# Another hand-written order for the first 18 head pairs of a fused attention and feed-forward kernel

## The chip, the core and the metric

The kernel runs on one core of a Trainium2 chip. A core has five engines that run their own instruction queues in order: TensorE (PE; its weight loads are shown as PEld), VectorE (DVE), ScalarE (ACT), GpSimd (POOL) and SyncE (SP, which here only issues DMAs). Matrix products are written to PSUM, a memory of eight banks; everything else lies in SBUF, 128 partitions wide. The metric is the time of one execution in microseconds (us).

## The reference

Cosine attention over 8 batches of 12 heads (448 tokens, 64 features a head), then a feed-forward layer on its result.

```python
q_n = q / (norm(q, axis=-1) + 1e-06)
k_n = k / (norm(k, axis=-1) + 1e-06)
attn = softmax((q_n @ k_n^T) / tau)          # tau = 0.1
x = (attn @ v), heads side by side           # 3584 x 768
h = x @ w_in                                 # 768 x 2048
out = (h * clip(h + 3, 0, 6) / 6) @ w_out    # 2048 x 768
```

## The kernel before

Two heads of one batch make a *pair* i (0 to 47), two pairs a *twin* d. What is loaded at a time is an *item* j: all q or all k of a twin, 128 partitions x 896 numbers (item 2d and 2d+1). Up to pair 17 everything that the program does stands in `PLAN` (L21 to L58), a list of lines of short codes; `run` (L959) takes them one by one and each code appends its instructions to the queue of its engine. So the list fixes the order within each engine's queue and nothing between engines, which wait for each other by semaphores alone. From pair 18 on a loop (L998 and following) writes the order; it is the same before and after.

The codes, with their lines:

- `LQ.j` loads an item, `LV.d` the values of a twin in four DMAs (both on SP). `W` (L909) issues one of eight loads of feed-forward weights, 768 KB each, from POOL's queue: four of w_in, then four of w_out.
- `SQ.j.e.c.n` squares n of an item's 7 columns (14 for items 0 and 1) on engine e: a is ACT (L222), v VectorE, p POOL (L224). `RE.j` adds the squares up (VectorE, L236). `NO.d` (L252 to L255) makes 1/(norm + 1e-6) of a twin in four small ACT operations: ln, exp(0.5 x), ln(x + 1e-6), exp(-x). `NM.j.e` multiplies the item by it and writes bf16 (L267). Squares lie in two buffers: items j and j+2 share one.
- `TR.j` turns an item in seven TensorE transposes into a bank (L312); from item 14 on `XD.j` does it by DMA (L323). `CQ.i`, `CK.i`, `CS.i` copy a pair's q, its k and the k of the last 64 tokens to where the score product reads them (L334 on VectorE, L332 on ACT, L362 on VectorE and L372 on POOL for DMA-turned items).
- `SC.i.g` is a group of score products (L412, L415), four groups a pair: three of 2 x 448 columns and a smaller one. `EX.i.g` is exp of it on ACT (L433). `VC.i` casts the values (L286, or L284 on VectorE as a reduction over one element), `VA.i.g` multiplies them with the exponentials into the bank pair PV (L455), and `FI.i` divides by the sums (VectorE, L475 and L476). `BK.i` and `CX.i` turn the result and copy it to the feed-forward input xT; `XB` and `XP` do it by DMA.
- `U` (L932) issues TensorE's next feed-forward unit from a list of 36: thirty of six products with w_in (L566, `mm1_unit`) and six output units of sixteen products with w_out (L613, `mm2_unit`). `UA` and `UV` issue the ACT and the VectorE part that follow a unit (L575, L581, L624, L626); the last of them gives the unit's bank back.
- `WS.x` adds or subtracts blocks of w_out (VectorE, L688). The sums 1, 6 and 7 have tiles of their own; y3 and y4 overwrite w_out in place, so they come after the sums that read it and after the output units. The products of the loop need them.
- `D.n` and `DP.n` issue n products with zeros, of 512 columns into bank Y (L916) and of 248 columns into an unused part of PV (L921). Nothing reads them.
- `OPEN` changes the PSUM layout: up to there scores alternate between two two-bank tiles; behind it scores, units, transposes and `BK` take banks in turn from a ring of six. An operation that takes a bank waits until whoever read it last is done.

Of the kernel before, what the change touches and what calls it, by code (L numbers as in the profile page):

```python
# [10 lines left out]
AF = mybir.ActivationFunctionType  # L11
# [3 lines left out]
EPS = 1e-6  # L15
# [3 lines left out]
ORDER = "111111111111111111111111111111222222"  # L19

PLAN = [  # L21
# [36 lines left out]
]  # L58


# [1 line left out]
def kernel(  # L62
# [10 lines left out]
    nc = tc.nc  # L73
    B, H, S, D = q.shape
# [29 lines left out]
    KC = FCN // 2  # L104
# [34 lines left out]
    def raw_buffer(j):  # L139
# [4 lines left out]
    n2s = [const.tile([128, 2, 14], FP32, name=f"n2{i}", tag=f"n2{i}") for i in range(2)]  # L144
    rs = [
        [const.tile([128, 2, 14], FP32, name=f"{x}{i}", tag=f"{x}{i}") for x in ("ln", "nr", "le", "r")]
        for i in range(2)
    ]
# [13 lines left out]
    engines = {"v": nc.vector, "p": nc.gpsimd, "a": nc.scalar, "s": nc.sync}  # L162
    issued = set()

    def needs(*what):
        for w in what:
            assert w in issued or any(x < 0 for x in w[1:] if isinstance(x, int)), w
# [76 lines left out]
    def norms(d, *items):  # L244

        needs(("NM", 2 * d - 4), ("NM", 2 * d - 3))
        items = items or (0, 1)
        for x in items:
            needs(("RE", 2 * d + x))
        it = slice(items[0], items[-1] + 1)  # L250
        ln, nr, le, r = (t[:, it, :] for t in rs[d % 2])
        nc.scalar.activation(out=ln, in_=n2s[d % 2][:, it, :], func=AF.Ln)  # L252
        nc.scalar.activation(out=nr, in_=ln, func=AF.Exp, scale=0.5)
        nc.scalar.activation(out=le, in_=nr, func=AF.Ln, bias=EPS)
        nc.scalar.activation(out=r, in_=le, func=AF.Exp, scale=-1.0)  # L255
        for x in items:
            issued.add(("NO", d, x))

# [411 lines left out]
            return wide[n % 2], wide[2]  # L670
        return wide_late[2 * (n - LOOP) : 2 * (n - LOOP) + 2]

    def weight_sums(what, c0, n):

        w = w_out_sb[:, :, :].rearrange("p (c k) m -> p c k m", k=2)[:, c0 : c0 + n]
        b11, b12, b21, b22 = (w[:, :, k, m] for k in range(2) for m in (LEFT, RIGHT))
        for x in {"y3": "16", "y4": "17"}.get(what, ""):
            assert all((x, c) in summed for c in range(c0, c0 + n))
        o, x, y, op = {
            "1": (b11, b11, b22, ALU.add),  # L680
            "6": (b11, b11, b12, ALU.add),
            "7": (b21, b21, b22, ALU.add),
            "y3": (b12, b12, b22, ALU.subtract),
            "y4": (b21, b21, b11, ALU.subtract),
        }[what]
        if what in w_sum:
            o = w_sum[what][:, c0 : c0 + n, :]
        nc.vector.tensor_tensor(out=o, in0=x, in1=y, op=op)  # L688
        summed.update((what, c) for c in range(c0, c0 + n))

    def half(b, t, k):
# [247 lines left out]
    def whole_units(n, engines="av"):  # L939
# [4 lines left out]
                    finish_units(e)  # L944

    OPS = {
        "LQ": load_qk, "LV": load_v, "W": next_weights, "SQ": square, "RE": reduce, "NO": norms,
        "NM": normalise, "VC": vcast, "TR": transposes, "XD": crossbar, "XB": back_crossbar, "XP": back_two, "CQ": copy_q, "CK": copy_k, "CS": copy_k3, "SC": scores,
        "EX": exps, "VA": values, "FI": finish_values, "BK": back, "CX": copy_x, "U": unit, "UA": lambda: finish_units("a"), "UV": lambda: finish_units("v"),
        "GL": g_left, "WS": lambda x, *h: weight_sums(str(x), *((h[0] * KC // 2, KC // 2) if h else (0, KC))), "UU": whole_units, "D": busy, "DP": busy_pv, "OPEN": open_ring,  # L950
    }

    def do(op, *args):
        OPS[op](*args)
        key = (op,) + tuple(a for a in args if isinstance(a, int))
        if op not in ("RE", "NM", "LQ"):
            issued.add(key[:3] if op == "SC" else key)

    def run(text):  # L959
# [36 lines left out]
    for i in range(FIRST, NP):  # L996
# [36 lines left out]
        n = 2  # L1033
# [59 lines left out]
```

## Time and profile before

| what | us |
|---|---|
| median of 3 runs (405.66 to 406.52) | 406.1 |
| the profiled execution | 405.02 |
| its span, first to last instruction | 403.2 |
| PE busy | 394.5 |
| VectorE / ACT / POOL busy | 286.4 / 266.2 / 233.2 |
| 86 zero products `DP`, between 2.5 and 41.6 | 13.3 by their durations, which overlap |
| 10 zero products `D`, from 5.71 | 2.3 |
| first exponential / first feed-forward unit start | 12.11 / 42.1 |
| last output unit of the planned part ends | 114.3 |

The granted TensorE clock was 1.00 in every stretch. Durations of PE overlap, since products are pipelined: the distance between two starts is the price of one. On the other engines the distance between two starts is a little below a duration as well. A line of the timeline gives start, length, engine, line, operation, output and input tiles, count, and in brackets the idle time before it with what ended it. A line of the waits gives who waited for whom, the total, the number of times and the longest.

### The profile page before, as it was taken

Reading aid. Unit: us, or ns where it says so; the run is one execution under the profiler, and the core shown is the slowest. Engines: PE = TensorE matmul, PEld = TensorE weight load, DVE = VectorE, ACT = ScalarE, POOL = GpSimd, SP = SyncE. Lnnn points to the kernel's source line nnn. Section 1 sums busy time; section 2 is a strip of 40 time slices with the busy share of each in tenths; the row PEclk is TensorE's granted clock in tenths of the full one; section 3 lists DMA queues with packets and bytes.
Section 4 is the critical chain, followed back from the end, with each engine's and each line's share of the span. In section 5 each row is a group of like instructions: output and inputs, shape, how many; then the busy total and the mean of one; then the engine's idle time right before and its main releaser. Section 6 shows DMA issues by size and latency. Waiting matters only on the chain.

```text
span 403.2 us, 9617 instructions
## 1 busy us (share of the span) xinstructions
PE 394.5 (98%) x3696; PEld 233.7 (58%) x3696; DVE 286.4 (71%) x501; ACT 266.2 (66%) x609; POOL 233.2 (58%) x228
## 2 busy tenths in 40 slices
PE   7999999999989999999999999999999999999996
PEld 5666556555655556555555556555565556555564
DVE  6898768766998676776857878687656666644663
ACT  6899998787557686776758768668648755224230
POOL 7899664562294996489386875776665500510070
PEclk9999999999999999999999999999999999999999
DMA  8999989989989559885989659986864523130133
GB/s 290 308 241 276 200 249 239 144 126 221 193 204 231 120 119 228 176 224 130 181 214 210 134 143 171 183 193 145 191 150 82 112 46 67 40 79 20 27 73 99
DMA packets 91566, 65.32 MB, mean 162 GB/s; under 512 B 56064, under 2 KB 89984, under 8 KB 91520
## 3 DMA queue, kind: packets, MB, share of 16 engines
q1 hardware_dynamic: 87408, 58.02, 62.8%
q0 software_dynamic: 3712, 6.29, 9.1%
q8 instruction: 29, 0.48, 0.5%
q10 hardware_dynamic: 400, 0.39, 0.3%
q14 instruction: 17, 0.14, 0.1%
HBM read 47.19 MB, written 11.01 MB: 144 GB/s over the span
## 4 chain that ended last, share of the span: by engine, by line
PE 94%; DVE 3%; DMA 1%; POOL 1%; ACT 0%; issue 0%; SPq 0%; DVEq 0%
PE M L566 24%; PE M L739 17%; PE PV L455 13%; PE Y L566 6%; PE M L415 6%; PE Z L566 5%; PE Y L739 4%; PE Z L739 4%; PE M L613 3%; PE M L819 2%; PE Z L415 2%; PE PV L921 2%; PE Z L819 1%; PE Y L415 1%; PE SC L415 1%; DMA big<-in_q_dram 1%
## 5 line engine op out<-in xcount | busy, mean ns | idle before, releaser
L433 ACT ACTIVATE at<-M 128x448 bf16<-128x448 f32 x200 | 99.6, 565 | 17.7 <-PE M L415 15.5
L566 PE MATMUL M<-xT,w_in_sb 128*128 128x448 bf16 x522 | 110.7, 353 | 0.0
L566 PEld LDWEIGHTS <-w_in_sb 128*128 128x128 bf16 x768 | 71.9, 98 | 62.5 <-issue 2.6
L267 POOL TENSOR_TENSOR nrm<-big,r 128x896 bf16<-128x896 f32 (+1 forms) x48 | 79.4, 1658 | 26.7 <-ACT r L255 18.5
L581 DVE SCALAR_TENSOR_TENSOR gT<-u,M 128x448 bf16<-128x448 bf16 x76 | 46.8, 618 | 35.6 <-ACT u L575 35.3
L455 PEld LDWEIGHTS <-at 128*128 128x128 bf16 (+1 forms) x1536 | 54.8, 97 | 24.1 <-issue 14.8
L224 POOL TENSOR_TENSOR big<-big 128x896 f32<-128x896 f32 (+3 forms) x39 | 63.8, 1639 | 8.0 <-DMA big<-in_k_dram 4.1
L575 ACT ACTIVATE u<-M 128x448 bf16<-128x448 f32 x87 | 48.8, 561 | 29.5 <-PE M L566 29.1
L455 PE MATMUL PV<-vx,at 128*128 128x65 bf16 (+1 forms) x1536 | 64.3, 194 | 0.2 <-DVE on L476 0.2
L236 DVE TENSOR_REDUCE n<-big 128x14 f32<-128x896 f32 (+1 forms) x50 | 51.8, 1040 | 3.9 <-ACT big L222 3.4
L372 POOL COPY km<-tT 64x128 bf16<-64x128 bf16 x34 | 12.4, 364 | 59.3 <-DMA tT<-nrm 43.4
L768 POOL TENSOR_TENSOR big<-big 128x384 f32<-128x384 f32 x11 | 12.0, 1088 | 55.1 <-ACT big L787 55.0
L739 PEld LDWEIGHTS <-gT 128*128 128x128 bf16 x288 | 27.8, 98 | 20.2 <-DVE gT L717 0.6
L739 PE MATMUL M<-w_out_sb,gT 128*128 128x384 bf16 x208 | 37.9, 326 | 0.1
L433 ACT ACTIVATE at<-Z 128x448 bf16<-128x448 f32 x49 | 27.6, 564 | 10.4 <-PE M L415 8.8
L286 POOL CAST vx<-big 128x512 bf16<-128x512 f32 x44 | 33.0, 754 | 2.4 <-DMA big<-in_v_dram 2.4
L476 DVE TENSOR_TENSOR on<-PV,rc 128x512 bf16<-128x512 f32 x48 | 33.2, 691 | 1.7
L415 PE MATMUL M<-tT,kz 64*128 64x448 bf16 (+1 forms) x175 | 31.9, 351 | 1.0 <-DVE o L626 1.0
L739 PEld LDWEIGHTS <-gs 128*128 128x128 bf16 x224 | 21.6, 98 | 14.5
L566 PE MATMUL Y<-xT,w_in_sb 128*128 128x448 bf16 x132 | 28.6, 353 | 0.0
L433 ACT ACTIVATE at<-Y 128x448 bf16<-128x448 f32 x45 | 25.6, 568 | 3.3 <-PE Z L415 3.1
L739 PE MATMUL M<-w_sum,gs 128*128 128x384 bf16 x144 | 26.3, 326 | 0.0
(131 smaller groups left out, 553.9 us busy)
## 6 DMA issues: line engine op xcount, KB each, us to landing
big<-in_v_dram SPq DMA_DIRECT2D x96, 128.0 KB, 4.7
big<-in_k_dram SPq DMA_DIRECT2D x24, 448.0 KB, 4.9
big<-in_q_dram SPq DMA_DIRECT2D x24, 448.0 KB, 4.3
out_dram<-o SPq DMA_DIRECT2D x107, 96.0 KB, 2.2
w_in_sb<-in_moe_w_in_dram POOLq DMA_DIRECT2D x4, 768.0 KB, 9.1
w_out_sb<-in_moe_w_out_dram POOLq DMA_DIRECT2D x4, 768.0 KB, 9.7
tT<-nrm SPq DMA_TRANSPOSE x34, 3.4
xT<-on SPq DMA_TRANSPOSE x25, 3.8
```

Of the source, the lines that this page charges most:

```text
L224: engines[e].tensor_tensor(out=o, in0=i, in1=i, op=ALU.mult)
L236: nc.vector.tensor_reduce(out=n2s[d % 2][:, j % 2, c], in_=sq[:, :, :, :].rearrange("p g c d -> p (g c) d")[:, c, :], axis=AX.X, op=ALU.add,)
L267: engines[e].tensor_tensor(out=nrm[:, :, g, :].rearrange("p c g d -> p g c d"), in0=raw_of[j][:, g, :, :], in1=rs[d % 2][3][:, j % 2, :] . ...
L286: (engines[e].copy if e == "a" else engines[e].tensor_copy)(out=o, in_=f)
L415: nc.tensor.matmul(o, ks, qt[rows], start=True, stop=True)
L433: nc.scalar.activation(out=o, in_=x, func=AF.Exp, scale=inv_tau)
L455: nc.tensor.matmul(pv_out(j, h), at[rows, n, q_cols(i // HP, j)], vt[rows, 3 + h if name == "M" else 5 * h + int(name[1]), :], start=(name ...
L476: nc.vector.tensor_tensor(out=on[:, :, :, :].rearrange("p j h d -> p h j d"), in0=pv4[:, :, :, 0:D], in1=rc[:, :, :].to_broadcast([128, 2, ...
L566: nc.tensor.matmul(ps[:, 0:S], w_in_sb[:, cc, fc * 128 : (fc + 1) * 128], x[:, cc, 0:S], start=(cc == 0), stop=(cc == CC - 1),)
L575: nc.scalar.activation(out=u[:, :], in_=ps[:, 0:S], func=AF.Relu, bias=0.5, scale=1.0 / 6.0)
L581: nc.vector.scalar_tensor_tensor(out=g[:, fc, c0 : c0 + S], in0=u[:, :], scalar=1.0, in1=ps[:, 0:S], op0=ALU.min, op1=ALU.mult,)
L739: nc.tensor.matmul(m, lhs[:, c, :], rhs[:, c, c0 : c0 + width], start=(base is None and c == 0), stop=(c == KC - 1), skip_group_check=True,)
```

## The change

`PLAN` is written anew, 37 lines for 36: the same steps for pairs 0 to 17 in another order, and in part on other engines or in other pieces.

- Zero products `DP`: 64 for 86, all of them ahead of `SC.2.0`; the group `D.10` opens the list.
- Squares: 30 pieces for 29 (11, 15 and 4 on ACT, POOL and VectorE for 12, 14 and 3). Item 1 is squared whole on ACT, item 0 by ACT (9 columns) and POOL (5); items 4, 7 and 10 go to VectorE; item 14 is squared in seven pieces of one column on three engines.
- Twins 2 to 6 get `NA.d` (the first two ACT operations of `NO`: ln, exp) and `ND.d` (an addition of 1e-6 and a reciprocal, on VectorE). They are new functions.
- Three of the four half normalisations of items 0 and 1 go to VectorE, and item 13's; items 2 and 18 return to POOL.
- On ACT instead of VectorE or POOL: four `CK`, five `CQ`, one `CS`, three `CX` (one, one, none and one before), and three casts `VC`; ten casts on POOL for sixteen.
- Of the weight sums, `WS.1` and `WS.7` and `WS.6` are made in halves, one half of each on POOL; y3 in two halves on VectorE.
- `TR.10` stands before the first `U`; `SC.17.3` behind the last.

The functions and the plan, the old one cut to its first lines and to those of its end:

```diff
 PLAN = [
-    "LQ.1 DP.5 SQ.1.a.11.3 SQ.1.p.4.3 DP.1 SQ.1.a.0.4 LQ.0 SQ.0.p.8.6 DP.2 DP.4 LQ.3 LQ.2 SQ.1.v.7.4 RE.1.1",
-    "SQ.0.a.0.6 RE.1.0 NO.0.1 LQ.5 LQ.4 SQ.0.v.6.2 DP.6 SQ.3.a.0.7 NM.1.p.0 D.10 RE.0.1 DP.3 NM.1.p.1 RE.0.0 DP.8",
-    "NO.0.0 LV.0 DP.2 SQ.2.a.0.7 NM.0.p.0 RE.3 RE.2 NM.0.p.1 TR.1.Y DP.2 TR.0.Z CK.0.v DP.4 SQ.4.p.0.7 CQ.0.v",
...
-    "CK.17.v XD.18 U EX.16.1 SQ.20.a.0.7 NM.19.p FI.15 WS.6 U UV XD.19 SC.16.3 RE.20 GL.0 WS.1 WS.7.0 EX.16.2 U VA.16.0 UA VA.16.1 LV.11",
-    "EX.16.3 SC.17.0 UV VC.19.p SC.17.1 SC.17.2 SQ.22.v.0.7 VA.16.2 LQ.23 EX.17.0 VA.16.3 EX.17.1 LV.10 U SC.17.3",
-    "XP.14 NO.10 FI.16 NM.20.p CK.18.v U CK.19.v WS.7.1 WS.y3 WS.y4.0 XB.16 EX.17.2 UV UA VA.17.0 VC.18.p EX.17.3 RE.22 CS.18.v",
+    "D.10 DP.9 LQ.1 SQ.1.a.0.14 DP.10 LQ.0 LQ.3 LQ.2 SQ.0.p.9.5 RE.1.1 SQ.0.a.0.9 RE.1.0 RE.0.1 RE.0.0 NO.0.1",
+    "DP.10 NM.1.v.0 NM.1.v.1 NO.0.0 NM.0.p.0 NM.0.v.1 TR.1.Y LQ.5 TR.0.Z DP.7 SQ.3.a.0.7 SQ.2.a.0.7 RE.3 DP.5",
+    "SQ.5.p.0.7 CK.1.a CK.0.a RE.2 CQ.0.a CQ.1.a NO.1 SC.0.0.0 SC.0.1.1 EX.0.0 NM.2.p NM.3.p DP.8 EX.0.1 SC.0.2.0",
+    "LQ.4 DP.6 LV.0 SC.0.3.1 DP.1 EX.0.2 SQ.4.v.0.7 RE.5 SC.1.0.0 TR.2.Z EX.0.3 RE.4 LQ.7 NA.2 VC.1.v EX.1.0",
+    "SC.1.1.1 VC.0.v VA.0.0 EX.1.1 LQ.6 TR.3.Y SQ.6.a.0.7 ND.2 SQ.7.v.0.7 SC.1.2.0 VA.0.1 VA.0.2 EX.1.2 NM.4.p",
+    "CQ.2.v LV.1 CK.2.v SC.1.3.1 NM.5.p CK.3.a VA.0.3 CQ.3.v DP.8 RE.6 LQ.8 EX.1.3 SC.2.0.0 FI.0 SC.2.1.1 LQ.9",
+    "EX.2.0 TR.4.Y VA.1.0 SC.2.2.0 VA.1.1 VC.2.v VA.1.2 EX.2.1 EX.2.2 SQ.8.p.0.7 LQ.10 RE.7 VA.1.3 VC.3.p",
+    "SQ.9.p.0.7 SC.2.3.1 SC.3.0.0 FI.1 NA.3 CQ.4.a TR.5.Z EX.2.3 ND.3 SC.3.1.1 VA.2.0 EX.3.0 EX.3.1 SC.3.2.0 RE.8",
+    "W VA.2.1 CQ.5.v VA.2.2 EX.3.2 CK.4.v SC.3.3.1 BK.0.Y SC.4.0.0 SQ.10.v.0.7 EX.3.3 VA.2.3 CX.0.v EX.4.0",
+    "SC.4.1.1 EX.4.1 SC.4.2.0 CK.5.v LV.2 EX.4.2 NM.6.p VC.4.p FI.2 VA.3.0 TR.6.Y NM.7.p VA.3.1 RE.9 NA.4 RE.10",
+    "SC.4.3.1 SC.5.0.0 VA.3.2 CQ.6.v EX.4.3 VA.3.3 BK.2.Z LQ.11 SC.5.1.1 CQ.7.v CX.2.v SQ.11.p.0.7 BK.1.Y EX.5.0",
+    "SC.5.2.0 FI.3 TR.7.Z EX.5.1 SC.5.3.1 CX.1.v CK.6.v CK.7.v ND.4 EX.5.2 EX.5.3 CS.7.v VA.4.0 OPEN BK.3.Y LV.3",
+    "CS.6.v SC.6.0 VA.4.1 W VA.4.2 CX.3.a VA.4.3 SC.6.1 SC.6.2 NM.8.p LV.4 EX.6.0 TR.8 VC.5.p SC.6.3 FI.4 VA.5.0",
+    "RE.11 CQ.9.v EX.6.1 EX.6.2 CQ.8.v BK.4 SC.7.0 VA.5.1 VA.5.2 NM.9.p EX.6.3 VA.5.3 NA.5 CX.4.v EX.7.0 SC.7.1",
+    "ND.5 VC.6.p SC.7.2 EX.7.1 EX.7.2 TR.9 SC.7.3 FI.5 NM.10.p BK.5 VA.6.0 W VA.6.1 EX.7.3 CK.8.v VA.6.2 SC.8.0",
+    "CK.9.v VA.6.3 EX.8.0 CS.8.v CX.5.v CS.9.v VC.7.v TR.10 CQ.10.v SC.8.1 SC.8.2 U EX.8.1 UA LQ.12 CQ.11.v",
...
+    "SC.10.3 VA.10.0 NA.6 EX.10.3 ND.6 LQ.17 U NM.13.v UA SQ.14.a.4.1 SQ.14.p.5.1 LQ.16 VA.10.1 SC.11.0 SC.11.1",
+    "SQ.14.a.3.1 U LV.6 NM.12.p UV EX.11.0 EX.11.1 UA VA.10.2 VA.10.3 SQ.14.p.2.1 BK.9 VC.11.v SC.11.2 U CX.9.a",
+    "SQ.14.p.1.1 SQ.14.a.0.1 TR.12 FI.10 UV TR.13 U UA W EX.11.2 BK.10 SQ.15.p.0.7 SC.11.3 SQ.14.v.6.1 W RE.14 UV",
...
+    "SQ.17.p.0.7 UV UA SC.13.0 NM.15.p NM.14.p WS.1.p.0 UV SC.13.1 EX.13.0 VA.12.2 UV W WS.7.p.0 SQ.18.a.0.7",
+    "LQ.20 VA.12.3 FI.12 U WS.6.v.0 XD.15 RE.17 UA LQ.19 UV XD.14 EX.13.1 SC.13.2 U LV.7 U UA EX.13.2 CK.14.v UA",
+    "UV U VC.15.p UV RE.18 NO.8 SC.13.3 U VA.13.0 U UA UV UA EX.13.3 SC.14.0 UA W UV NM.16.p EX.14.0 CS.14.v",
...
+    "UA NM.18.p SC.16.1 CS.16.v SC.16.2 VA.15.2 LV.9 EX.16.0 WS.1.v.1 VA.15.3 XD.18 EX.16.1 FI.15 U SC.16.3",
+    "EX.16.2 VA.16.0 NM.19.p EX.16.3 XD.19 VA.16.1 UV SC.17.0 SC.17.1 WS.7.v.1 WS.6.p.1 WS.y3.v.1 SC.17.2",
+    "SQ.22.p.0.7 EX.17.0 XP.14 VA.16.2 VC.19.p WS.y3.v.0 VA.16.3 U U FI.16 UA EX.17.1 RE.22 XB.16 EX.17.2 CK.18.v",
+    "LV.11 NM.20.p UV VC.18.a WS.y4.v.0 SC.17.3 CK.19.v CS.18.v EX.17.3 VA.17.0",
 ]
...
+    def powers(d, *items):
...
+        ln, nr = (t[:, it, :] for t in rs[d % 2][:2])
+        nc.scalar.activation(out=ln, in_=n2s[d % 2][:, it, :], func=AF.Ln)
+        nc.scalar.activation(out=nr, in_=ln, func=AF.Exp, scale=0.5)
...
+    def reciprocals(d, *items):
...
+        nr, le, r = (t[:, it, :] for t in rs[d % 2][1:])
+        nc.vector.tensor_scalar_add(out=le, in0=nr, scalar1=EPS)
+        nc.vector.reciprocal(out=r, in_=le)
...
-    def weight_sums(what, c0, n):
+    def weight_sums(what, c0, n, e="v"):
...
-        nc.vector.tensor_tensor(out=o, in0=x, in1=y, op=op)
+        engines[e].tensor_tensor(out=o, in0=x, in1=y, op=op)
```

More of the change, by code (lines that the diff above doesn't have):

```diff
@@ L255, in norms @@
         nc.scalar.activation(out=r, in_=le, func=AF.Exp, scale=-1.0)
+        for x in items:
+            issued.add(("NO", d, x))
+    def powers(d, *items):
+        needs(("NM", 2 * d - 4), ("NM", 2 * d - 3))
+        items = items or (0, 1)
+        for x in items:
+            needs(("RE", 2 * d + x))
+        it = slice(items[0], items[-1] + 1)
+        ln, nr = (t[:, it, :] for t in rs[d % 2][:2])
+        nc.scalar.activation(out=ln, in_=n2s[d % 2][:, it, :], func=AF.Ln)
+        nc.scalar.activation(out=nr, in_=ln, func=AF.Exp, scale=0.5)
+        for x in items:
+            issued.add(("NA", d, x))
+    def reciprocals(d, *items):
+        items = items or (0, 1)
+        for x in items:
+            needs(("NA", d, x))
+        it = slice(items[0], items[-1] + 1)
+        nr, le, r = (t[:, it, :] for t in rs[d % 2][1:])
+        nc.vector.tensor_scalar_add(out=le, in0=nr, scalar1=EPS)
+        nc.vector.reciprocal(out=r, in_=le)
         for x in items:
@@ L946 @@
     OPS = {
-        "LQ": load_qk, "LV": load_v, "W": next_weights, "SQ": square, "RE": reduce, "NO": norms,
+        "LQ": load_qk, "LV": load_v, "W": next_weights, "SQ": square, "RE": reduce, "NO": norms, "NA": powers, "ND": reciprocals,
         "NM": normalise, "VC": vcast, "TR": transposes, "XD": crossbar, "XB": back_crossbar, "XP": back_two, "CQ": copy_q, "CK": copy_k, "CS": copy_k3, "SC": scores,
         "EX": exps, "VA": values, "FI": finish_values, "BK": back, "CX": copy_x, "U": unit, "UA": lambda: finish_units("a"), "UV": lambda: finish_units("v"),
-        "GL": g_left, "WS": lambda x, *h: weight_sums(str(x), *((h[0] * KC // 2, KC // 2) if h else (0, KC))), "UU": whole_units, "D": busy, "DP": busy_pv, "OPEN": open_ring,
+        "GL": g_left, "WS": lambda x, e, *h: weight_sums(str(x), *((h[0] * KC // 2, KC // 2) if h else (0, KC)), e), "UU": whole_units, "D": busy, "DP": busy_pv, "OPEN": open_ring,
     }
@@ L955, in do @@
         key = (op,) + tuple(a for a in args if isinstance(a, int))
-        if op not in ("RE", "NM", "LQ"):
+        if op not in ("RE", "NM", "LQ", "NA", "ND"):
             issued.add(key[:3] if op == "SC" else key)
```

41 rows, old and new, of the table PLAN are left out of this document.

## The prediction

> **What bounds the kernel now.** I read the page first, then the table of stretches, then the waits of PE and the timelines of the other engines. The page has PE at 98% of the span, so at first sight TensorE is the bound:
>
> ```profile
> PE 394.5 (98%) x3696; PEld 233.7 (58%) x3696; DVE 286.4 (71%) x501; ACT 266.2 (66%) x609; POOL 233.2 (58%) x228
> PEclk9999999999999999999999999999999999999999
> ```
>
> That share hides one stage. The table of stretches (busy us per engine), cut where the first feed-forward unit starts (42.1 us) and where the planned part ends (about 117 us), shows it:
>
> ```profile
> 0.00:12.00 12.00, 8.81 (x65) 6.12 (x65) 8.36 (x31) 7.60 (x19) 9.40 (x24) 1.00 0.89 284
> 12.00:42.00 30.00, 29.57 (x421) 19.44 (x417) 25.97 (x60) 28.53 (x57) 28.34 (x23) 1.00 1.07 276
> 42.00:75.00 33.00, 33.00 (x345) 19.19 (x344) 24.09 (x49) 28.80 (x67) 18.23 (x18) 1.00 1.04 216
> 75.00:100.00 25.00, 25.00 (x249) 14.00 (x248) 17.50 (x31) 20.09 (x49) 11.87 (x15) 1.00 0.91 161
> 100.00:117.00 17.00, 15.99 (x141) 9.58 (x140) 16.60 (x18) 9.29 (x23) 9.19 (x7) 1.00 0.92 216
> ```
>
> From 12 to 42 us ACT is busy 28.53 of 30 us and POOL 28.34, and PE's 29.57 holds about 49 zero products. So the start is set by the three helper engines; from 42 us on PE never waits and sets the time, until one wait near 115 us. PE's waits in all:
>
> ```profile
> PE PV L921 <- DVE vx L972: 2.5, 1, 2.5
> PE M L415 <- DVE o L626: 1.0, 1, 1.0
> PE Z L312 <- POOL nrm L267: 0.7, 1, 0.7
> PE PV L455 <- DVE on L476: 0.2, 1, 0.2
> ```
>
> The 1.0 is a score product waiting for a bank whose store stands on VectorE behind two weight differences. The same rows carry a second fact. In VectorE's and GpSimd's timelines:
>
> ```profile
> 100.21 2.65 DVE L688 TENSOR_TENSOR w_sum<-w_out_sb 128x3072 bf16<-128x3072 bf16 x1
> 111.34 4.52 DVE L688 TENSOR_TENSOR w_out_sb<-w_out_sb 128x3072 bf16<-128x3072 bf16 x2
> 115.79 0.54 DVE L626 COPY o<-M 128x384 f32<-128x384 f32 x1
> ```
>
> ```profile
> 99.56 1.68 POOL L267 TENSOR_TENSOR nrm<-big,r 128x896 bf16<-128x896 f32 x1
> 101.19 2.14 POOL L286 CAST vx<-big 128x512 bf16<-128x512 f32 x1
> 112.92 2.14 POOL L286 CAST vx<-big 128x512 bf16<-128x512 f32 x1
> ```
>
> A cast that takes 0.61 elsewhere takes 2.14 while VectorE adds weights, and the weight sum begun at 100.21 takes 2.65 although a normalisation held POOL until 101.24: 1.0 of waiting and 1.65 of work. Two-input operations of VectorE and operations of POOL take turns.
>
> **The sum's base.** The profiled execution took 405.02 us (span 403.2, 1.8 outside); the runs' median is 406.1, 1.1 above. I add differences to the median. A difference under 0.2% (0.8 us) can't be told from none here; the chances use that bound.
>
> **Zero products.** 22 of 86 go. Warm, 13 took 1.37 us (7.87 to 9.24), 0.105 each: 2.3 us of PE. They lie between 2.5 and 42 us, where PE waits for ACT's exponentials, so I take 0; the ends are 0 and -2.3. The D group of ten goes ahead of all, into the 2.48 to 9 us in which PE has nothing else: 0. If that cover were gone it would cost its 2.16 us (5.71 to 7.87).
>
> **First twin.** Item 1's squares are one ACT operation of 896 (0.93 by its row) instead of three pieces: 4.24 to 5.17, reductions (0.54 apart) to 6.35, r at 7.36 against 6.90 before. But the normalisations, four on POOL in 3.64 before, go three to VectorE (1.08 for 896, so 0.54 each) and one to POOL (0.91): TR.0 at 9.5 to 10.0, not 10.67. ACT then has two squares (0.84 each), four copies of transposes (0.44 each, new on ACT) and NO.1 (0.9) ahead of the first exponential: 8.3 + 1.7 + 1.75 + 0.9 = 12.65 against 12.11. So +0.55: the gain at the transposes is spent in ACT's queue.
>
> **From there to the first unit.** ACT's work through EX.8.0 before: 8 pairs of exponentials 23.0 (2.84 each, 3.0 for the two with split banks), EX.8.0 0.86, four NO 3.9, one square 0.84: 28.6 in 30.1 elapsed. After: four NA at 0.49 for the four NO (-1.9), three copies more (+1.35): 28.05. Alone that puts EX.8.0's end at 12.65 + 28.05 = 40.7 plus idle time. But VectorE has now: ten reductions of 1.0, three squares of 1.0 (SQ.4, 7, 10; one normalisation before), three casts 0.6, fourteen copies 0.3, six FI of 0.85, CX 2.0, four CS of 0.45, four ND at about 0.4 (no row has one; between two 0.06 memsets and two 0.21 reciprocals, taken near the latter because the second waits for the first): 29.5 us from 9.35, so 38.9 without one gap. I walked its queue in order: it waits 0.9 for NA.2 (ND.2 at 16.4), 0.4 for SQ.6, 0.4 for VA.1.3, and RE.10 ends at 30.65. NA.4, behind EX.4.2 (done 30.2), waits for it and holds EX.4.3 for 0.5. ND.4 ends at 34.3, and NM.8, TR.8 follow at 36.05; RE.11 at 37.7, NA.5 38.5, ND.5 38.9, FI.5 40.05, CX.5 41.65, CS.9 42.1; CS.9 frees the bank of SC.8.1, and the first unit starts at 42.75, not 42.09: +0.65 (the +0.55 is in it). If SQ.10 on VectorE (25.7) must wait for NM.6 on POOL (24.8 to 26.45) all behind it moves 0.75 more; if VectorE's gaps don't reach ACT, it is -0.95 (the first rival). TR.10 (7 transposes, 0.41) is done before the first unit instead of behind it: -0.41.
>
> On the ND pair one rule speaks against the change. The Trainium skill, SBUF — State Buffer, section "Who interferes with whom", says that a tensor_scalar can take the 2-port mode and then locks against any GpSimd operation for its whole length. By it each of the five ND adds could wait out a POOL operation of 1.65, an estimate of at most 8 us, if all met one; no row before has such an add. By my walk POOL is idle or waiting for that very ND in three of five, so I leave the sum as it is.
>
> **Queues moved past.** SP: LQ.7, now ahead of LQ.6, waits for NM.0 (9.4; LQ.7 went out at 11.96 before); LV.2 is issued behind LQ.10 at 16.8 to 19.4 and LQ.11 right after, against VC.4 at 26.5 and SQ.11 at 29.7, with 4.7 to 4.9 to landing: 0. XD.15 and XD.14 go out at 72 to 74, CK.14 runs at 81: 0. POOL: the second w_in chunk (W) stands behind SQ.11, which needs RE.9: issued at 31.3, not 28.0. The four chunks landed 8.4 to 12.2 after issue, so 39.7 to 43.5 against 42.75: 0 likely, +0.75 the end, +2.2 if SQ.10 is held too.
>
> **Units, 42 to 114 us.** PE's work is the same piece by piece (36 units, 69 VA, the rest), 71.9 us by the pitches (1.135 a unit, 2.6 an output unit, 0.29/0.195 SC, 0.25 VA). New on POOL are three half weight sums of 1536 elements: 1.89 ns an element by the squares (1691 for 896) gives 2.9, by the 384-element additions (1088) 4.4; I take 2.9, the row nearer in size. WS.7.p.0 runs at about 80 to 83 and holds CK.14 on VectorE, behind which the bank releases of units 22 and 23 stand; SC.14.0 needs them at 85.8. The eighth W, behind that sum and a cast that waits for LV.7, is issued at 84 and lands 7.2 to 7.7 later, at 91 to 92; the first output unit starts at 92 and reads that chunk last (94). Seven single-column pieces of SQ.14 cost ACT 0.3 each where it is busy 28.8 of 33: hidden. I take +0.4 for all, between 0 and +3 (both sums at 4.4).
>
> **End of the plan.** Removed: the 1.01 wait, since the store now stands ahead of y4's first half. Added: SC.17.3 moved behind the last unit, so VA.17.3 waits for EX.17.3: +0.45. That would be -0.55. But from 98.6 on POOL has NM.18, CS.16, NM.19, WS.6 half, SQ.22, VC.19, NM.20: 10.8 us, and VectorE five weight halves (1.0 or 1.3) and copies: 6.7. Taking turns they fill 98.6 to 116. Walked in order: WS.7's half waits for SQ.22 until 108.3, y3's halves end at 111.15 and 114.1, FI.16 at 114.95 and CK.18 at 116.25, where SC.18.0 (before at 114.64, with the 1.0 still to come) needs it. That is +0.6; with turns that fall well -0.55, with 4.4 us for the half sum +2.1. I take +0.6.
>
> **Sum:** +0.65 - 0.41 + 0.4 + 0.6 = +1.24: 407.3 us, 0.3% slower.
>
> **Rivals.** *ScalarE was the limit* (faster): the halved norms free ACT, VectorE's gaps stay short, the first unit starts 0.95 earlier (40.7 + 0.55 idle = 41.25 against 42.21 for EX.8.0's end); with TR.10 and -0.55 at the end that is -1.9: 404.2. For it: ACT's 28.53 of 30. Against: VectorE's 29.5. It decides if the stretch from EX.0.0 to EX.8.0's end is under 29.3 us. *Nothing to tell* (same): my walk of the start, no held bank, turns fall well: +0.65 - 0.41 - 0.55 = -0.3: 405.8. *Long POOL sums and a late chunk*: +3 in the units and +2.1 at the end in place of 0.4 and 0.6, in part: about 410. *The clock*: after SC.2.0 (20 us) no zero product stands by, and PE's real work is some 80% of 20 to 42 us. A cold PE shows in the first 18 zero products, 3.40 us or 0.19 each; 3.4 us at that pace would add up to 2 us: 409.3. Against: gaps under 1 us. The Trainium skill, TensorE: Matmul & The Clock Gate, section "What's actually happening", has the clock halve only after a whole idle window of about 3.4 us; no gap of my walk is so long.
>
> **Chances.** Forecast 0.40 (406.9 to 409), long sums 0.08, clock 0.03: slower 0.51. Same 0.22. Faster 0.27. The range reaches to the faster rival and to the long sums: 404.2 to 410.
>
> **What would show it.** The first unit (L566) at 42.7 in the changed trace, EX.0.0 at 12.7; ACT waiting for n2 or VectorE at NA.4; PE's waits without the bank store but with at from ACT and kz or on from VectorE near 114; POOL's weight sums near 2.9. Wrong would make me a first unit before 41.5, or no PE wait after 100 us.

## The result and the profile after

| | before | after |
|---|---|---|
| median, us | 405.97 | 411.61 (410.71 to 413.74) |
| ratio, with its 95% interval | | 1.0154 (1.0134 to 1.0175) |
| profiled execution / its span | 405.02 / 403.2 | 410.71 / 408.9 |
| first feed-forward unit starts | 42.09 | 47.53 |

The change costs 1.5%. The sign of the forecast was right; the time lies above its range. The lines of after's page that answer to those of before:

```profile
PE 394.4 (96%) x3674; PEld 233.5 (57%) x3674; DVE 296.2 (72%) x506; ACT 269.2 (66%) x612; POOL 237.1 (58%) x224
PEclk9996999999999999999999999999999999999999
```

PE's busy time is about that of before (394.5), with 22 fewer zero products and some products at a lower clock; the span grew by waiting. And the granted clock, 9 in every slice before, has a 6 in the fourth. The table of stretches, in the columns of before (busy us of PE, PEld, DVE, ACT, POOL, then the clock, the DMA share and GB/s):

```profile
12.00:42.00 30.00, 24.23 (x314) 15.81 (x311) 26.93 (x49) 24.23 (x45) 21.08 (x17) 0.89 0.94 228
42.00:75.00 33.00, 31.05 (x378) 18.85 (x376) 28.37 (x61) 27.08 (x65) 17.19 (x16) 1.00 0.97 210
100.00:117.00 17.00, 17.00 (x187) 10.78 (x186) 12.15 (x17) 11.58 (x29) 12.05 (x9) 1.00 0.92 218
```

In the stretch to 42 us PE fell from 29.57 busy to 24.23, ACT from 28.53 to 24.23 and POOL from 28.34 to 21.08: there these three now wait, and of VectorE's 26.93 some 2.7 is a square that was blocked (below). From 100 to 117 us PE has no gap left, where it had 1.01. PE's waits, from the longest down:

```profile
PE PV L481 <- DVE on L502: 3.4, 1, 3.4
PE Y L942 <- DVE vx L998: 2.5, 1, 2.5
PE SC L441 <- ACT at L459: 1.6, 4, 0.5
PE M L592 <- DVE gT L607: 1.5, 1, 1.5
```

The 2.5 is in both kernels. New are the 3.4, at the second half of FI.2 (L502), and the 1.5, a unit that waits for its bank. Their places on PE's timeline:

```profile
28.24 0.36 PE L441 MATMUL SC<-tT,kz 64*128 64x448 bf16 x2 [0.36 <-ACT at L459]
31.96 0.62 PE L481 MATMUL PV<-vx,at 128*128 128x65 bf16 x8 [3.35 <-DVE on L502]
32.39 0.94 PE L338 MATMUL Y<-ident,nrm 128*128 128x128 bf16 x7
...
47.53 1.31 PE L592 MATMUL M<-xT,w_in_sb 128*128 128x448 bf16 x6
...
73.42 1.29 PE L592 MATMUL M<-xT,w_in_sb 128*128 128x448 bf16 x6 [1.50 <-DVE gT L607]
```

What VectorE did while PE waited, with the later place (69 us) and, for comparison, a weight sum at 109 us:

```profile
23.56 1.27 DVE L280 TENSOR_SCALAR le<-nr 128x28 f32<-128x28 f32 x1
...
26.71 3.75 DVE L225 TENSOR_TENSOR big<-big 128x896 f32<-128x896 f32 x1
...
31.21 0.69 DVE L502 TENSOR_TENSOR on<-PV,rc 128x512 bf16<-128x512 f32 x1
31.82 2.07 DVE L237 TENSOR_REDUCE n<-big 128x14 f32<-128x896 f32 x2
...
69.13 2.50 DVE L225 TENSOR_TENSOR big<-big 128x128 f32<-128x128 f32 x1
...
109.07 2.36 DVE L714 TENSOR_TENSOR w_sum<-w_out_sb 128x1536 bf16<-128x1536 bf16 x1
```

GpSimd at the same places:

```profile
25.61 1.70 POOL L293 TENSOR_TENSOR nrm<-big,r 128x896 bf16<-128x896 f32 x1
27.25 0.61 POOL L312 CAST vx<-big 128x512 bf16<-128x512 f32 x1
27.82 1.68 POOL L293 TENSOR_TENSOR nrm<-big,r 128x896 bf16<-128x896 f32 x1
32.97 1.68 POOL L225 TENSOR_TENSOR big<-big 128x896 f32<-128x896 f32 x1 [3.47 <-DVE n L237]
...
68.93 0.82 POOL L935 DMA_DIRECT2D w_out_sb<-in_moe_w_out_dram  x1
69.77 1.69 POOL L225 TENSOR_TENSOR big<-big 128x896 f32<-128x896 f32 x1
...
108.94 1.69 POOL L293 TENSOR_TENSOR nrm<-big,r 128x896 bf16<-128x896 f32 x1
110.58 3.81 POOL L714 TENSOR_TENSOR w_sum<-w_out_sb 128x1536 bf16<-128x1536 bf16 x1
```

SQ.10, which takes 1.03 us alone (SQ.7 at 16.74), stood 3.75: from its issue at 26.71 GpSimd ran NM.6, the cast VC.4 and NM.7 without a gap until 29.50, and the square ended at 30.46, 0.96 later. Behind it on VectorE stood FI.2, which gives PE its bank back, and the sums of item 9. ScalarE shows the second victim:

```profile
27.27 2.54 ACT L459 ACTIVATE at<-SC 128x896 bf16<-128x896 f32 x3 [0.38 <-PE SC L441]
32.93 0.23 ACT L268 ACTIVATE ln<-n 128x28 f32<-128x28 f32 x1 [3.12 <-DVE n L237]
```

NA.4 waited 3.12 us for those sums, with the exponentials behind it. And in the gap on PE the clock fell, in windows of 5 us and then cut at the end of PE's last product and at the fall:

```profile
25.00:30.00 5.00, 2.85 (x38) 1.55 (x36) 5.00 (x5) 4.43 (x6) 4.48 (x4) 1.00 0.90 174
30.00:35.00 5.00, 3.04 (x33) 2.19 (x34) 4.45 (x9) 1.13 (x4) 2.03 (x2) 0.54 0.94 230
35.00:40.00 5.00, 4.93 (x73) 3.35 (x70) 3.28 (x14) 3.99 (x7) 1.01 (x2) 0.78 0.84 137
...
28.61:30.41 1.80, 0.00 (x0) 0.00 (x0) 1.80 (x2) 1.20 (x2) 0.89 (x1) 1.00 1.07 192
30.41:37.23 6.82, 5.27 (x55) 3.64 (x55) 5.01 (x12) 2.37 (x5) 2.32 (x2) 0.50 0.78 172
```

The balance: first unit +5.44 (42.09 to 47.53), TR.10 already done -0.41, waits in the units +1.8 (1.5 and 0.3), the wait at 115 us gone -1.0: +5.8, against +5.7 of span and +5.6 of the medians.

### The profile page after: what moved, and what is told of

It is laid out like the page before. It is cut to its first block, busy times and chain, and to the rows that moved or that the text cites. A ratio compares the mean times of both kernels' runs of the same rounds, so it can differ in the third digit from the quotient of the medians.

```text
span 408.9 us, 9592 instructions
## 1 busy us (share of the span) xinstructions
PE 394.4 (96%) x3674; PEld 233.5 (57%) x3674; DVE 296.2 (72%) x506; ACT 269.2 (66%) x612; POOL 237.1 (58%) x224
## 4 chain that ended last, share of the span: by engine, by line
PE 89%; DVE 7%; ACT 3%; issue 1%; DVEq 0%
PE M L592 22%; PE M L765 17%; PE PV L481 12%; PE Y L592 6%; PE M L441 5%; PE Z L592 5%; PE Y L765 4%; PE Z L765 4%; PE M L639 3%; PE M L845 2%; ACT at L459 2%; DVE big L225 1%; PE Z L639 1%; PE Z L845 1%; PE Z L441 1%; PE Y L441 1%
## 5 line engine op out<-in xcount | busy, mean ns | idle before, releaser
L592 PE MATMUL M<-xT,w_in_sb 128*128 128x448 bf16 x510 | 108.1, 353 | 1.5 <-DVE gT L607 1.5
L293 POOL TENSOR_TENSOR nrm<-big,r 128x896 bf16<-128x896 f32 (+1 forms) x46 | 80.9, 1760 | 14.8 <-DVE r L281 4.5
L225 POOL TENSOR_TENSOR big<-big 128x896 f32<-128x896 f32 (+2 forms) x40 | 62.6, 1567 | 25.8 <-DMA big<-in_k_dram 9.1
L607 DVE SCALAR_TENSOR_TENSOR gT<-u,M 128x448 bf16<-128x448 bf16 x74 | 45.3, 617 | 32.1 <-ACT u L601 31.9
L601 ACT ACTIVATE u<-M 128x448 bf16<-128x448 f32 x85 | 47.6, 562 | 28.0 <-PE M L592 27.6
L502 DVE TENSOR_TENSOR on<-PV,rc 128x512 bf16<-128x512 f32 x48 | 33.2, 691 | 1.9 <-DVE rc L501 0.2
L592 PE MATMUL Y<-xT,w_in_sb 128*128 128x448 bf16 x150 | 32.4, 352 | 0.0
L312 POOL CAST vx<-big 128x512 bf16<-128x512 f32 x38 | 26.1, 690 | 6.4 <-DMA big<-in_v_dram 6.2
```

The lines of the kernel that those rows point to most:

```text
L225: engines[e].tensor_tensor(out=o, in0=i, in1=i, op=ALU.mult)
L293: engines[e].tensor_tensor(out=nrm[:, :, g, :].rearrange("p c g d -> p g c d"), in0=raw_of[j][:, g, :, :], in1=rs[d % 2][3][:, j % 2, :] . ...
L312: (engines[e].copy if e == "a" else engines[e].tensor_copy)(out=o, in_=f)
L502: nc.vector.tensor_tensor(out=on[:, :, :, :].rearrange("p j h d -> p h j d"), in0=pv4[:, :, :, 0:D], in1=rc[:, :, :].to_broadcast([128, 2, ...
L592: nc.tensor.matmul(ps[:, 0:S], w_in_sb[:, cc, fc * 128 : (fc + 1) * 128], x[:, cc, 0:S], start=(cc == 0), stop=(cc == CC - 1),)
L601: nc.scalar.activation(out=u[:, :], in_=ps[:, 0:S], func=AF.Relu, bias=0.5, scale=1.0 / 6.0)
```

## The experiments

The theory: SQ.10 on VectorE is blocked for as long as GpSimd has work ready, and what it costs is what stands behind it on VectorE. The rivals: the cold clock, for want of zero products; the norms split between two engines; and GpSimd's longer queue, so that another placing of the square would be late too. All ratios are against the kernel before, run on the same chip; the changed kernel's own is 1.0154.

**The square left out.**

```diff
+        if j == 10:
+            return
```

> The changed kernel without the one square of item 10 (it is left out; its sum then adds up older squares). Theory A (the square on VectorE stood 2.7 us behind GpSimd and, with its own 1.0, made PE wait 3.35 us and the clock fall): the wait of PE for on goes, the clock stays 1.00 between 30 and 40 us, the first unit starts at 42.5 to 44 instead of 47.5, and the time falls by 3.5 to 5 us, to 406.5 to 408. Theory B (the clock alone, for want of zero products): without the wait no idle window, so the clock holds too, but the time falls by only the clock's share, some 2 us. Theory C (the split norms hold the start): not more than 1 us.

Measured: 406.48 us, ratio 1.0017 (0.9995 to 1.0038). The wait at PV is gone, the clock is 1.00 in every stretch, and the first unit starts as soon as its weights are there:

```profile
43.88 1.29 PE L594 MATMUL M<-xT,w_in_sb 128*128 128x448 bf16 x6 [1.47 <-DMA w_in_sb<-in_moe_w_in_dram]
```

One square of 1.03 us carries nearly the whole loss (1.0154 to 1.0017). The run leaves out the square's own work as well as its wait. What then holds the first unit is the second chunk of w_in: the unit starts 12.3 us after that chunk's issue at 31.56.

**Thirty zero products behind FI.2.**

```diff
-    ... FI.2 VA.3.0 TR.6.Y NM.7.p ...
+    ... FI.2 DP.30 VA.3.0 TR.6.Y NM.7.p ...
```

> The changed kernel with 30 zero products more (3.1 us of PE) just ahead of VA.3.0, where PE waits 3.35 us. Theory A: the wait of the helpers is untouched; only the slow products after it get faster: 32.0 to 36.6 us held 2.5 us of work at full pace, so 1.5 to 2.1 us at most, 409.5 to 410. Theory B: the clock stays 1.00 and nearly the whole loss of the start, 3 us or more, comes back. If the time stays at 411 or rises, the clock cost nothing that the helpers did not cost anyway.

Measured: 415.1 us, ratio 1.0256 (1.0212 to 1.0301). They did not fill the gap: zero products write into PV, so they too waited for FI.2 (3.35 us) and then ran at 0.19 each, 5.8 us more on PE. This tests only that a filler which needs the late bank is no filler.

**Twenty-two zero products ahead of FI.2.**

```diff
-    "SC.4.1.1 EX.4.1 SC.4.2.0 CK.5.v ...
+    "SC.4.1.1 EX.4.1 SC.4.2.0 DP.22 CK.5.v ...
```

> The changed kernel with 22 zero products more behind SC.4.2.0 and ahead of FI.2 in the program, so that they need not wait for FI.2 as the 30 of the run before did (those began at 31.8, with FI.2, and took 5.7 us at 0.19 each). They fill 28.6 to 30.9 of the 3.35 us in which PE waits. Theory A: the helpers' delay stays, the clock stays 1.00 through 30 to 40 us and the products from 32.0 to 36.6 take their 2.5 us: first unit at 45.5 to 46.5 instead of 47.5, 409.5 to 410.3. Theory B: 3 us or more come back, 408.6 or less. Rival: clock back and no time, 411 to 412.

Measured: 411.03 us, ratio 1.0143 (1.0119 to 1.0167). The stretch that had 0.54 now has a full clock:

```profile
30.00:35.00 5.00, 3.42 (x47) 2.93 (x45) 4.97 (x7) 1.21 (x3) 1.53 (x2) 1.00 1.06 228
```

The time hardly moved: the intervals of the two kernels overlap, and the medians differ by 0.6 us. The profiled execution started 2 us late (a load of keys was late, GpSimd waited 2.69 for it) and its square waited longer than in after, so the price of the clock by itself isn't isolated; that a full clock doesn't bring the 5.6 us back is shown.

**The norms unsplit.** `NO` for `NA` in twins 2 to 6, and no `ND`:

```diff
-    "... RE.4 LQ.7 NA.2 VC.1.v EX.1.0",
-    "... SQ.6.a.0.7 ND.2 SQ.7.v.0.7 ...
+    "... RE.4 LQ.7 NO.2 VC.1.v EX.1.0",
+    "... SQ.6.a.0.7 SQ.7.v.0.7 ...
```

> The changed kernel with all four steps of the norms of twins 2 to 6 on ACT again (NO where NA stood, no ND). Theory C (the split holds the start): 1.5 to 3 us faster, since the 1.27 us and 0.56 us additions leave VectorE. Theory A: the square of item 10 then starts at about 25.3, and if it gets in ahead of NM.6 (25.6) the time falls by 3 to 4; if the DMA issue and NM.6 still hold it, the time falls by 0 to 1. If the split was a gain in itself, the time rises by up to 1.

Measured: 411.32 us, ratio 1.0149 (1.0127 to 1.0171). The square came earlier (26.09) and was blocked longer (4.52). The split is not the cause.

**The last column of item 14 on ScalarE.**

```diff
-    "... SC.11.3 SQ.14.v.6.1 W RE.14 UV",
+    "... SC.11.3 SQ.14.a.6.1 W RE.14 UV",
```

> The changed kernel with the one column of item 14's square that VectorE did (2.50 us for 128 elements) done by ACT at the same place. Theory A: PE's 1.50 us wait before L592 at 72 to 73.4 goes and the time falls by 1.2 to 1.5. Rival: the wait comes back at the next bank and the time falls by less than 0.5.

Measured: 411.04 us, ratio 1.0144 (1.0115 to 1.0174). PE's wait at the unit fell from 1.5 to 0.9 us, not to zero: the sums RE.14 now wait for ScalarE, and the unit's part (UV), which gives the bank back, still stands behind them.

**The cast behind the second normalisation.**

```diff
-    ... NM.6.p VC.4.p FI.2 VA.3.0 TR.6.Y NM.7.p VA.3.1 ...
+    ... NM.6.p FI.2 VA.3.0 TR.6.Y NM.7.p VC.4.p VA.3.1 ...
```

> The changed kernel with the cast VC.4 on GpSimd behind NM.7 instead of between NM.6 and NM.7. If a waiting VectorE operation gets its turn as soon as GpSimd's running one ends, the square ends near 28.4 instead of 30.4 and 2 us or more come back. If GpSimd keeps its turn as long as its queue has ready work, the square ends with NM.7 or the cast (30 to 31) and the time stays within 0.7 us of 411.6.

Measured: 411.73 us, ratio 1.015 (1.0128 to 1.0173). VectorE's square, and GpSimd in another order:

```profile
27.52 3.74 DVE L225 TENSOR_TENSOR big<-big 128x896 f32<-128x896 f32 x1
```

```profile
26.42 3.34 POOL L293 TENSOR_TENSOR nrm<-big,r 128x896 bf16<-128x896 f32 x2
29.70 0.61 POOL L312 CAST vx<-big 128x512 bf16<-128x512 f32 x1
```

The square ended at 31.26, 0.95 after the cast. A normalisation behind NM.6 kept the square out as the cast had: at this place it made no difference which of the two came next.

**Three places mended, the square on GpSimd.** The second `W` is issued with the first, and item 14's column goes to ScalarE with UV ahead of RE.14:

```diff
-    "W VA.2.1 ... SQ.10.v.0.7 EX.3.3 ...
+    "W W VA.2.1 ... SQ.10.p.0.7 EX.3.3 ...
-    "... SC.6.0 VA.4.1 W VA.4.2 ...
+    "... SC.6.0 VA.4.1 VA.4.2 ...
-    "... SC.11.3 SQ.14.v.6.1 W RE.14 UV",
+    "... SC.11.3 SQ.14.a.6.1 W UV RE.14",
```

> The changed kernel with three steps moved: item 10's square on GpSimd at the same place, the second w_in load right behind the first (its late landing held the first unit for 1.47 us in the run without the square), and item 14's column on ACT with one bank release ahead of the sum that waits for it. Theory A: all of PE's waits of the changed kernel but the unavoidable start go; first unit near 42.4 to 43, no wait at 72; 5.1 + 1.5 + 1.2 less than 411.6 is 403.8, with 402.8 to 405 as bounds: the rest of the order is worth some 0.2 to 0.6% against the kernel before. Rival: GpSimd's queue, 1.65 us longer, makes NM.6 and the items behind it late, and the start keeps 1 us or more of the loss: 405.5 or more.

Measured: 406.54 us, ratio 1.0013 (0.9991 to 1.0035); no new wait of PE is longer than 0.64 us, and the first unit starts at 43.68, with PE busy up to it. The 5 us are back with the square still done, on the engine that blocked it. The square's move was not run alone; the run with the two other places mended and the square on VectorE (below) stays at 1.0076, so they alone don't do it. It doesn't beat the kernel before, and what the trace shows of the rival is that NM.6 now ends at 30.46, not 27.31, and that PE waits 0.64 for it.

**Before, with its last 22 zero products taken out** (64 left, as after has; all `DP` from pair 1's last scores on):

```diff
-    "DP.2 SC.1.3.1 EX.1.2 ... DP.3 SC.2.0.0 DP.2 EX.1.3 ...
+    "SC.1.3.1 EX.1.2 ... SC.2.0.0 EX.1.3 ...
```

> The kernel before without its last 22 zero products (64 left, all ahead of SC.2.0, as in the changed kernel). If they only filled waits: the same time within 0.3%, clock 1.00. If they held the clock: a stretch under 1.00 between 20 and 42 us and 1 to 3 us more. If they stood on PE's path: up to 1.7 us less (17 of them at 0.10 behind SC.2.0).

Measured: 404.95 us, ratio 0.999 (0.9969 to 1.0012). No cost and no gain can be told: the interval leaves room for 0.3% less and 0.1% more. From 20 us on the clock is 1.00 without them. (Before that it fell to 0.83 and 0.82 in two windows of 5 us, after a gap of 1.96 on PE in an execution that started late; the run of the plan's end alone, below, has all the products and 0.91 and 0.75 there.)

**The square later: behind FI.2.**

```diff
-    "... BK.0.Y SC.4.0.0 SQ.10.v.0.7 EX.3.3 ...
-    "... NM.6.p VC.4.p FI.2 VA.3.0 ...
+    "... BK.0.Y SC.4.0.0 EX.3.3 ...
+    "... NM.6.p VC.4.p FI.2 SQ.10.v.0.7 VA.3.0 ...
```

> The changed kernel with item 10's square (SQ.10, 128x896 on VectorE) moved in the list from ahead of the five operations that end before FI.2 to just behind FI.2. Theory A (what costs is that FI.2, and with it TensorE, stood behind a blocked square): FI.2 no longer waits, TensorE's wait of 3.4 us at PV is gone, the clock is 1.00 from 30 to 40 us, the first unit starts at 44 to 45 us, and the time is 2 to 5 us under the changed kernel's: 406.5 to 409.5. What stays late is item 10's norm on ScalarE. Rival (the square is late wherever it stands, and item 10's own chain through its norm and turn is what the first unit needs): the wait moves to TensorE's turn of item 10 or to a score behind it, and the time is within 1 us of 411.6.

Measured: 409.43 us, ratio 1.0088 (1.0052 to 1.0124): half of it. PE's wait for FI.2 is gone. (The profiled execution started late: VectorE waited 1.74 for a load of queries.)

**The square behind FI.2 and the two other places mended** (against the run before it; the later W is taken out of its old place):

```diff
-    "W VA.2.1 ...
+    "W W VA.2.1 ...
-    "... SC.11.3 SQ.14.v.6.1 W RE.14 UV",
+    "... SC.11.3 SQ.14.a.6.1 W UV RE.14",
```

> The changed kernel with three places mended: SQ.10 on VectorE behind FI.2 as in the run e9_later, the second chunk of w_in issued together with the first, and SQ.14's last column on ScalarE with the unit's bank store ahead of the root. Theory A, if its parts add (square behind FI.2: -2 to -5; second chunk: 0 to -1.5; column: -0.6 to -1.5): 403.5 to 409. If the other kernel that moved SQ.10 to GpSimd (406.5) was held by GpSimd's longer queue, this one ends below it, under 406; if what is left is TensorE's own work before the first unit, it ends at the same 406.5.

Measured: 409.52 us, ratio 1.0076 (1.0047 to 1.0105), no better than the run before it. Its start agrees with after's within 0.3 us, so its places can be compared. VectorE, then ScalarE and PE:

```profile
28.34 2.64 DVE L225 TENSOR_TENSOR big<-big 128x896 f32<-128x896 f32 x1
30.90 2.07 DVE L237 TENSOR_REDUCE n<-big 128x14 f32<-128x896 f32 x2
```

```profile
32.01 0.23 ACT L268 ACTIVATE ln<-n 128x28 f32<-128x28 f32 x1 [2.34 <-DVE n L237]
```

```profile
32.97 0.56 PE L441 MATMUL SC<-tT,kz 64*128 64x448 bf16 x2 [2.02 <-ACT at L459]
```

The square met NM.7 (28.34 to 30.02) and waited 1.6. The victim is now the sums of item 9, with NA.4 and the exponentials behind them.

**And item 9's sums ahead of the square** (against the run before it).

```diff
-    ... FI.2 SQ.10.v.0.7 VA.3.0 TR.6.Y NM.7.p VA.3.1 RE.9 NA.4 RE.10",
+    ... FI.2 RE.9 SQ.10.v.0.7 VA.3.0 TR.6.Y NM.7.p VA.3.1 NA.4 RE.10",
```

> The kernel of the run e11_both with one operation moved: the row sums of item 9 (RE.9, VectorE) ahead of item 10's square instead of behind it. In e11_both ScalarE's norm NA.4 started at 32.01 us after 2.34 us of waiting for those sums, its EX of the next scores stood behind it, and TensorE waited 2.0 us for them at 32.97. Theory A in its final form (a blocked VectorE operation costs what stands behind it on VectorE, first FI.2 and then NA.4's sums; the square itself is not urgent): NA.4 starts near 29.5 us, TensorE's wait of 2.0 us is gone, the first unit starts at 44 us and not 46.10, and the time is 1.5 to 2.5 us under that run's 409.5: 407 to 408. Rival (item 10's square and its own norm and turn are what is late): the wait moves on by a step and the time stays within 0.7 us of 409.5.

Measured: 410.25 us, ratio 1.0091 (1.0057 to 1.0124): not what I expected. NA.4 did start early (30.65), and no time came of it. VectorE, GpSimd and PE:

```profile
30.44 3.94 DVE L225 TENSOR_TENSOR big<-big 128x896 f32<-128x896 f32 x1
```

```profile
29.54 0.62 POOL L312 CAST vx<-big 128x512 bf16<-128x512 f32 x1
30.11 1.69 POOL L293 TENSOR_TENSOR nrm<-big,r 128x896 bf16<-128x896 f32 x1
31.75 1.67 POOL L225 TENSOR_TENSOR big<-big 128x896 f32<-128x896 f32 x1
```

```profile
36.15 0.58 PE L519 MATMUL Y<-ident,on 128*128 128x128 bf16 x4 [3.79 <-DVE tT L360]
```

SQ.11 on GpSimd needs item 9's sums (items 9 and 11 share a buffer). With the sums early, SQ.11 was ready behind NM.7, and the square waited for it too: 2.9 us. The victim is the next in the queue, the copy of item 6's turn, and PE waited 3.79 for that bank. My expectation had counted what GpSimd held ready in the run before, not what the move would make ready.

**The end of the plan alone, in the kernel before.**

```diff
-    ... WS.7.1 WS.y3 WS.y4.0 XB.16 EX.17.2 UV UA ...
+    ... WS.7.1 WS.y3 XB.16 EX.17.2 UV WS.y4.0 UA ...
```

> The kernel before, with one entry of the last planned line moved: the bank store ahead of the half sum of the fifth shared piece (UV ahead of WS.y4.0) instead of behind it. If the prediction's end term is right (TensorE's 1.0 us wait at 115 us is for a bank that VectorE empties behind that half sum), the wait goes and the time falls by about 1.0 us to 404.6, ratio 0.9975. If the wait was a sum of several lateness, or what stands behind is late next, the ratio is within 0.001 of 1.

Measured: 405.62 us, ratio 0.9995 (0.9964 to 1.0026). The 1.0 us wait is gone from the trace, but the interval holds both answers: -1.0 us can't be told from nothing here. No run beats the kernel before by more than its interval.

## Why the prediction was right in sign and wrong in size

**The failing step** stands in the walk to the first unit: "If SQ.10 on VectorE (25.7) must wait for NM.6 on POOL (24.8 to 26.45) all behind it moves 0.75 more". The place was right, the price was not: the sum put this wait at nothing, the sentence at 0.75. It was 2.7 us, and the first unit came 3.65 later than without the square (43.88 to 47.53), 5.1 later if the chunk's 1.47 is taken off. The price came from "take turns", read from a weight sum that had waited for one normalisation only. A fuller table, of every run whose SQ.10 met GpSimd at work (us; the square alone takes 1.03):

| run | issued | GpSimd's last operation without a gap ends | the square ends |
|---|---|---|---|
| after | 26.71 | 29.50 (NM.6, cast, NM.7) | 30.46 |
| 30 zero products | 26.57 | 29.36 (NM.6, cast, NM.7) | 30.32 |
| item 14 on ScalarE | 26.57 | 29.37 (NM.6, cast, NM.7) | 30.32 |
| cast moved | 27.52 | 30.31 (NM.6, NM.7, cast) | 31.26 |
| norms unsplit | 26.09 | 29.66 (NM.6, cast, NM.7) | 30.61 |
| 22 zero products | 27.07 | 31.46 (W, NM.6, cast, NM.7) | 32.41 |
| behind FI.2 | 33.24 | 33.88 (NM.7) | 34.84 |
| behind FI.2, two mended | 28.34 | 30.02 (NM.7) | 30.98 |
| item 9's sums first | 30.44 | 33.42 (NM.7, SQ.11) | 34.38 |

The square ended 0.95 to 0.96 after GpSimd's run of ready operations in all nine, so here it got no turn, and the wait was as long as that run. The Trainium skill, SBUF — State Buffer, section "Who interferes with whom", has a VectorE instruction with two SBUF inputs contend with a GpSimd instruction that reads SBUF; the shared ports are an exclusive lock, and of a holder in a 2-port mode it says that it keeps them "for the whole instruction" while the other "fully blocks". That agrees with the full block (0.96 left of 1.03 is nearly all of the square's work), but read as one instruction it would give at most 1.7, and 2.7 to 4.3 were measured in the seven runs in which GpSimd had more than one operation left.

That the square gets no turn is no rule of the two engines, though. In the run with the square behind FI.2 alone, item 4's square, the same operation in the same size, did get in between two normalisations of GpSimd, whose input r was ready at 13.27:

```profile
13.45 1.69 POOL L293 TENSOR_TENSOR nrm<-big,r 128x896 bf16<-128x896 f32 x1
15.10 2.54 POOL L293 TENSOR_TENSOR nrm<-big,r 128x896 bf16<-128x896 f32 x1
```

```profile
13.51 2.58 DVE L225 TENSOR_TENSOR big<-big 128x896 f32<-128x896 f32 x1 [1.74 <-DMA big<-in_q_dram]
```

It ended at 16.09, 0.95 after the first of them, and the second took 2.54 for 1.69. In the run with 22 zero products it got in likewise, between SQ.5 and NM.2 (13.63 to 15.14). So "take turns" held there and failed for item 10's square; why is open.

**What the wait cost** was more than itself. FI.2 and the sums of item 9 stood behind the square, and both are at the head of chains: bank to PE (3.35 idle), sums to NA.4 to exponentials (3.12 idle). NA.4's wait I had priced at 0.5; FI.2 I had not priced at all. The placings show a chain of victims: ahead of FI.2 it was FI.2, behind it item 9's sums, behind those the copies of a turn; only on the other engine (with two other places mended) or left out did the loss go.

**The clock**, which I gave 0.03 with "gaps under 1 us", came in: 0.54 and 0.78 of full speed after one gap of 3.35. Seven transposes took 0.94 us there (32.39, in PE's timeline above), 0.56 at full clock (at 28.73 in the run with the square behind FI.2 and two places mended). The argument against it failed twice: PE's gap was 3.35, not under 1, and a shorter one is enough. The clock fell 1.8 us into the gap (0.50 from 30.41 on), and in other runs with gaps of 2.34 (norms unsplit, from 31.18 on) and 2.02 (behind FI.2, two mended, from 32.57 on); with one of 1.58 (22 zero products) it stayed. The Trainium skill, TensorE: Matmul & The Clock Gate, section "What's actually happening", puts the idle window at about 3.4 us; these traces don't agree with the prediction's reading that a whole window without work is needed. What the clock cost is not isolated: with it kept at 1.00 the median fell by 0.6 us, inside the intervals.

**Item 14's column**, "hidden" in my units term, was wrong in the same way: one column on VectorE stood 2.50 us at 69.13, behind the issue of a weight load and SQ.15 on GpSimd (it ended 0.17 after that), and held UV, for which PE waited 1.5 us. With the column on ScalarE PE still waited 0.9, since UV stands behind the sums there too. I had checked ScalarE's share of the pieces and not VectorE's one.

**The end** was +0.6 and came to -1.0: PE has no wait after 100 us, which I had named as a sign of being wrong. My walk had the weight halves and GpSimd's operations fill 98.6 to 116 us; the half on GpSimd waited 0.7 (3.81 for 3.1), the halves on VectorE went through in 2.36 and 1.98, and the store came at 114.39.

**The second chunk of w_in**: forecast to be issued at 31.3 and to land after 8.4 to 12.2 us. With the square gone it was issued at 31.56, the unit that needs it started 12.3 later, and PE waited 1.47: twice the 0.75 that I gave as the end for a square that isn't held (2.2 was for one that is), and the sum took 0. In after itself it was issued at 34.59, behind SQ.11, and hidden by the late start.

**The sign** owes something to luck. The units came to +1.8 where I had +0.4, the end to -1.0 where I had +0.6: two misses that nearly cancel. That the run without the square lies at +0.2%, near the forecast's +0.3%, is no confirmation of the sum.

**Right:** EX.0.0 at 12.65, seen at 12.92; the first unit without the blocked square at 42.75, seen at 42.41 plus the wait for the chunk, in a run that leaves out the square's own 1.03 too; zero products at nothing (ratio 0.999, within its interval); GpSimd's half sums at 2.9, seen at 3.09 and 3.10 where unblocked. The Trainium skill, SBUF — State Buffer, section "Who interferes with whom", has tensor_scalar among the operations that can contend with GpSimd; the ND adds agree (ND.3 took 1.27 us and ended 0.04 after GpSimd's square of item 9, ND.2 took 0.18). Leaving them out of the sum was right as far as can be told: without them the ratio is 1.0149.

## What to carry to other kernels

Before a two-input operation moves to VectorE, list what GpSimd will have ready at its issue and let the price range up to the end of that whole run, not of one operation (item 10's square waited it out nine times out of nine, item 4's got in earlier twice); then read down VectorE's own queue and price what stands behind. A move that makes a GpSimd operation ready earlier can lengthen that run. Here the square cost less in GpSimd's own queue, although it is slower on it (1.68 against 1.03).

## What was not expected of the hardware

- Item 10's fp32 square on VectorE found no turn between two GpSimd operations when the second was ready (seven runs, table above), while item 4's did in two runs, and so did bf16 weight sums: the one issued at 109.07 ended at 111.43, though GpSimd's next was ready at 110.63 and waited for it. So it isn't the type or the size alone that decides; what does stays open.
- The issue of a weight load on GpSimd can block as well: in the run with 22 zero products the square was issued at 27.07 with GpSimd only issuing W until 27.53 and NM.6 starting at 27.56; had it run beside W it would have ended at 28.1, and it ended at 32.41. At 69.13 the column met a W in the same way and waited. But it ended at 71.63, after SQ.15 and with the next W under way (71.40 to 72.21), so not every issue holds it.
- Loads of the first items landed about 2 us later in some profiled executions (GpSimd's SQ.5 began at 12.52, not 10.45, in the run with 22 zero products); two of them took 3.2 and 3.4 us over their kernel's median. Places in the first 45 us are compared here only between executions whose start agrees.
